# Evacuating the output with one 64-partition copy per engine, and storing it as 128 rows of 256 B

## The chip, the cores and the metric

One core of a Trainium2 chip. The metric is the device time of one execution in microseconds (us); a kernel's time is the median of its runs. TensorE multiplies, VectorE and ScalarE copy, and SyncE (SP) issues the loads and the store: the "issue" is its instruction that starts a transfer, the "landing" the transfer's last semaphore update. SBUF and PSUM are the core's own memories (the products end up in PSUM), DRAM is the memory outside it. Where a time is compared, it is with runs of the kernel before on the same chip in the same rounds.

## The reference, cut to what matters

One decoding step of attention for 32 sequences. Each reads the last 512 positions of its key and value caches, and the result goes through an output projection:

```python
q = (x @ wq) ...                       # x: [32, 1, 512]
p = softmax(q . k * Dh**-0.5)          # 8 kv heads, 512 positions, Dh = 128
o = p . v
return o.reshape(32, 1, 4096) @ wo     # out: [32, 1, 512] in bf16, 32 KB
```

The kernel reads 75.5 MB and writes 32 KB. The change is about these 32 KB.

## The kernel before: the parts that matter

```python
oT_flat = oT_sb[:, :, :].rearrange("p h b -> p (h b)")
x_sb = oT_flat[0:32, 0:D]
out_sb = x_sb.rearrange("b (c n) -> b c n", c=4)      # 32 partitions x 4 x 128
...
# SyncE (SP): the last loads, then the store
for hg in range(NHG):
    sp.dma_start(wo_sb[:, hg]..., wo[...]...).then_inc(sem_wo[hg], 16)
sp.wait_ge(dve_out, 2)
sp.wait_ge(act_out, 2)
sp.dma_start(out.rearrange("b s n -> b (s n)"),
             out_sb[:, :, :].rearrange("b c n -> b (c n)")).then_inc(sem_out, 16)
sp.wait_ge(sem_out, 16)
...
# TensorE: four column tiles, so output columns 128c .. 128c+127 land on partitions 32c .. 32c+31
for hg in range(NHG):
    pe.wait_ge(sem_wo[hg], 16)
    for i in range(4):
        for c in range(4):
            ins = pe.matmul(X_ps[32*c:32*(c+1), 2, 0:128], lhsT=o_sel[:, i, hg, :],
                            rhs=wo_sb[:, hg, i, c*128:(c+1)*128], ..., tile_position=(0, 32*c))
ins.then_inc(pe_fin, 1)
...
# VectorE; ScalarE does the same for c = 2, 3 with activation(Copy)
dve.wait_ge(pe_fin, 1)
for c in range(2):
    dve.tensor_copy(out_sb[:, c, :], X_ps[32*c:32*(c+1), 2, 0:128]).then_inc(dve_out, 1)
```

The four copies do two things: they bring the result out of PSUM, and they move the four groups of 32 partitions next to each other, so that one sequence's 512 columns lie in one partition and the store has 32 rows of 1024 B.

## Time and profile before

| | before |
|---|---|
| time | 188.11 us (188.02 to 188.25, 3 runs); 188.06 over 6 runs |
| span of the profiled run | 185.9 us |
| end of the last product | 183.35 us |
| from there to the end ("the tail") | 2.60 us |

The prediction shows the slices, the end of the chain, the timeline of the tail and the issue times. Two more lines of the page are needed. The first counts all DMA packets (its counts "under" a size are cumulative), the second is the store: kilobytes, and us from the start of the issue to landing.

```profile
DMA packets 6160, 75.80 MB, mean 408 GB/s; under 512 B 704, under 2 KB 768, under 8 KB 1792
...
out_dram<-oT_sb SPq DMA_DIRECT2D x1, 32.0 KB, 1.5
```

The 704 packets under 512 B are all semaphore writes of 4 B, 16 for each of 44 transfers. The packet records do not name a DMA engine; as in the prediction, 16 such writes are taken to stand for 16 engines.

### The profile page before, as it was taken

To read this page: it belongs to the slowest core of one execution; us is meant where nothing else is said; L and a number is where in the kernel's file an instruction comes from. 1 tells how busy PE (TensorE), PEld (TensorE's weight loads), DVE (VectorE), ACT (ScalarE), POOL (GpSimd) and SP (SyncE) were. 2 spreads that over 40 slices of the span, in tenths; PEclk is the share of its full clock that TensorE was granted. 3 is DMA by queue.
4 is the path that set the end of the run, shared out by engine and by line. 5 is a ranking of instruction groups with operands and counts; after the bars stand their busy time and mean duration, and the time that the engine had idled before them with its cause. 6 is when DMAs were issued, how large, how long until landed. Compare 5 with 4: busy or idle time off the path is not lost.

```text
span 185.9 us, 3841 instructions
## 1 busy us (share of the span) xinstructions
PE 110.3 (59%) x1604; PEld 90.7 (49%) x1604; DVE 131.8 (71%) x239; ACT 82.4 (44%) x142; POOL 32.1 (17%) x82
## 2 busy tenths in 40 slices
PE   0232004346179925949726992459699975999851
PEld 0100001032069804929326881129669974999741
DVE  0006999689999799985899959999999993010001
ACT  3001000259420199011992039826989999711011
POOL 7100390500700071050420060000030000000000
PEclk9999999999999995796955899657999999699999
DMA  6999999999999999999999999999999999999980
GB/s 208 419 444 423 430 430 419 444 423 426 426 419 430 426 419 430 434 419 434 418 430 430 423 434 412 441 430 416 432 416 430 423 430 426 423 430 404 401 326 25
DMA packets 6160, 75.80 MB, mean 408 GB/s; under 512 B 704, under 2 KB 768, under 8 KB 1792
## 3 DMA queue, kind: packets, MB, share of 16 engines
q1 hardware_dynamic: 6096, 75.53, 96.2%
q8 instruction: 12, 0.20, 0.4%
q10 hardware_dynamic: 48, 0.03, 0.1%
q14 instruction: 4, 0.03, 0.0%
HBM read 75.53 MB, written 0.03 MB: 406 GB/s over the span
## 4 chain that ended last, share of the span: by engine, by line
DMA 58%; DVE 22%; PE 11%; issue 4%; SPq 3%; ACT 0%; DVEq 0%
DMA V_sb<-in_v_cache_dram 31%; DVE KT_sb L426 14%; DMA w_sb<-in_wo_dram 12%; DMA K_sb<-in_k_cache_dram 8%; PE O_ps L353 7%; DMA w_sb<-in_wq_dram 6%; DVE w_sb L448 4%; DVE QA_sb L416 2%; PE S_ps L316 2%; SPq L211 2%; PE X_ps L296 1%; PE PT_ps L335 1%; SPq L200 1%; DVE oT_sb L409 0%; DVE KT_sb L404 0%
## 5 line engine op out<-in xcount | busy, mean ns | idle before, releaser
L426 DVE STREAM_TRANSPOSE KT_sb<-K_sb 128x2048 uint32<-128x2048 uint32 x32 | 72.3, 2287 | 1.2 <-DMA K_sb<-in_k_cache_dram 1.1
L353 PE MATMUL O_ps<-w_sb,V_sb 128*128 128x128 bf16 x640 | 46.1, 241 | 10.5 <-DMA V_sb<-in_v_cache_dram 5.6
L353 PEld LDWEIGHTS O_ps<-w_sb,V_sb 128*128 128x128 bf16 x640 | 44.7, 109 | 13.7 <-issue 7.0
L265 POOL COPY QBD<-QA_sb 32x64 bf16<-32x64 bf16 x64 | 25.6, 540 | 79.6 <-PE S_ps L316 62.0
L515 ACT ACTIVATE w_sb<-PTc,mask 128x512 bf16<-128x512 bf16 x60 | 38.9, 729 | 0.0
L316 PE MATMUL S_ps<-KT_sb,QBD 128*32 128x512 bf16 x256 | 20.9, 479 | 26.3 <-DVE KT_sb L426 19.8
L448 DVE TENSOR_SCALAR w_sb<-PTc,mask 128x512 bf16<-128x512 bf16 x100 | 30.2, 370 | 4.9 <-PE O_ps L353 4.9
L316 PEld LDWEIGHTS S_ps<-KT_sb,QBD 128*32 128x32 bf16 x256 | 7.8, 110 | 35.9 <-issue 32.0
L487 ACT ACTIVATE X_ps<-S_ps,negmax 128x512 f32<-128x512 f32 x8 | 5.3, 659 | 42.2 <-DVE negmax L435 42.2
L335 PE MATMUL PT_ps<-P_bf,pick 128*128 128x128 bf16 x128 | 11.8, 265 | 18.0 <-ACT P_bf L496 14.7
L335 PEld LDWEIGHTS PT_ps<-P_bf,pick 128*128 128x128 bf16 x128 | 10.2, 122 | 20.9 <-ACT P_bf L496 16.3
L525 ACT ACTIVATE oT_sb<-O_ps 128x128 bf16<-128x128 f32 x8 | 6.0, 750 | 26.0 <-PE O_ps L353 26.0
L515 ACT ACTIVATE K_sb<-PTc,mask 128x512 bf16<-128x512 bf16 x24 | 15.3, 717 | 1.6 <-DVE KT_sb L426 1.6
L353 PE MATMUL O_ps<-K_sb,V_sb 128*128 128x128 bf16 x256 | 15.1, 217 | 1.3 <-DMA V_sb<-in_v_cache_dram 1.0
L353 PEld LDWEIGHTS O_ps<-K_sb,V_sb 128*128 128x128 bf16 x256 | 14.5, 96 | 2.1 <-issue 1.3
L448 DVE TENSOR_SCALAR K_sb<-PTc,mask 128x512 bf16<-128x512 bf16 x40 | 12.1, 377 | 0.3 <-ACT PTc L506 0.2
L353 PE MATMUL O_ps<-KT_sb,V_sb 128*128 128x128 bf16 x128 | 9.1, 240 | 2.4 <-DMA V_sb<-in_v_cache_dram 2.4
L353 PEld LDWEIGHTS O_ps<-KT_sb,V_sb 128*128 128x128 bf16 x128 | 8.9, 108 | 2.5 <-issue 2.5
L469 DVE CAST K_sb<-S_ps 128x256 bf16<-128x256 f32 x1 | 0.4, 424 | 12.7 <-PE S_ps L365 12.7
L515 ACT ACTIVATE KT_sb<-PTc,mask 128x512 bf16<-128x512 bf16 x12 | 7.8, 725 | 0.0
L467 DVE CAST K_sb<-X_ps 128x384 bf16<-128x384 f32 x1 | 0.6, 558 | 9.8 <-PE X_ps L365 9.8
L496 ACT ACTIVATE P_bf<-X_ps,recip 128x512 bf16<-128x512 f32 x8 | 5.5, 685 | 4.4 <-DVE recip L441 4.4
(41 smaller groups left out, 49.5 us busy)
## 6 DMA issues: line engine op xcount, KB each, us to landing
K_sb<-in_k_cache_dram SPq DMA_DIRECT2D x16, 2048.0 KB, 15.2
V_sb<-in_v_cache_dram SPq DMA_DIRECT2D x16, 2048.0 KB, 17.0
w_sb<-in_wq_dram SPq DMA_DIRECT2D x2, 2048.0 KB, 9.7
w_sb<-in_wo_dram SPq DMA_DIRECT2D x8, 512.0 KB, 20.3
oT_sb<-in_x_dram ACTq DMA_DIRECT2D x1, 32.0 KB, 4.5
out_dram<-oT_sb SPq DMA_DIRECT2D x1, 32.0 KB, 1.5
```

The costliest lines, as they stand in the source:

```text
L211: sp.dma_start(wo_sb[:, hg].rearrange("p i n -> p (i n)"), wo[hg * 512:(hg + 1) * 512, :].rearrange("(m i) n -> m (i n)", i=4),).then_inc( ...
L265: pool.tensor_copy(dst[:, i, :, x0:x0 + 4], src).then_inc(pool_qbd, 1)
L316: ins = pe.matmul(S_ps[32 * c:32 * c + 32, q % 2, :], lhsT=QBD[:, q % 2, g, b, e, :], rhs=bass.AP(tensor=KT_sb, offset=s0 * slot + (b * G ...
L335: ins = pe.matmul(PT_ps[:, r, :], lhsT=pick[:, r, KS - s:KS - s + P], rhs=P_bf[:, s, :], start=(s == 0), stop=(s == KS - 1), tile_position ...
L353: ins = pe.matmul(O_ps[:, q % 2, 0:P], lhsT=V_sb[:, m % NV, r, :], rhs=z_of(q)[:, :, x0 + r, :], start=(e == 0 and r == 0), stop=(e == 1 a ...
L416: dve.tensor_copy(QA[32 * a:32 * a + 32, c], QW[32 * c:32 * c + 32, :, :, a::4].rearrange("p h k q -> p h q k"),).then_inc(dve_q, 1)
L426: dve.transpose(KT_w[:, n % NK, b].rearrange("p i r s -> p r i s"), K_w[:, n % NK, :, 32 * b:32 * b + 32],).then_inc(dve_T, 1)
L448: ins = dve.tensor_scalar(z_of(q)[:, k].rearrange("p x r -> p (x r)"), PTc[:, q % RING].rearrange("p x r -> p (x r)"), mask[:, k:k + 1], N ...
L487: act.activation(P_f32, S_ps[:, q % 2, :], ACTF.Exp, bias=negmax[:, q:q + 1], scale=SCALE, accum_out=sums[:, q:q + 1],).then_inc(act_exp, 1)
L496: act.activation(P_bf[:, :, :], P_f32.rearrange("p (x s) -> p s x", s=KS), ACTF.Copy, scale=recip[:, q:q + 1],).then_inc(act_P, 1)
L515: ins = act.activation(z_of(q)[:, k].rearrange("p x r -> p (x r)"), PTc[:, q % RING].rearrange("p x r -> p (x r)"), ACTF.Copy, scale=mask[ ...
L525: act.activation(oT_sb[:, :, 4 * q:4 * q + 4].rearrange("p h a -> p a h"), O_ps[:, q % 2, 0:P].rearrange("p (a h) -> p a h", a=4), ACTF.Co ...
```

## The change

Its intent: each engine evacuates its two groups of 32 partitions with one operation of 64, since the copies of this trace take their time from the columns and not from the partitions (on VectorE 280 ns for 32 partitions by 128 columns, 291 ns for 128 by 128). The result then stays on 128 partitions, and the store has to put it in order: 128 rows of 256 B, with a DRAM side that counts c (4), then b (32).

```diff
-        out_sb = x_sb.rearrange("b (c n) -> b c n", c=4)
+        out_sb = oT_flat[:, 0:P]
@@
-            sp.wait_ge(dve_out, 2)
-            sp.wait_ge(act_out, 2)
+            sp.wait_ge(dve_out, 1)
+            sp.wait_ge(act_out, 1)
             sp.dma_start(
-                out.rearrange("b s n -> b (s n)"), out_sb[:, :, :].rearrange("b c n -> b (c n)")
+                out.rearrange("b s (c n) -> c b (s n)", c=4), out_sb
             ).then_inc(sem_out, 16)
@@
-            for c in range(2):
-                dve.tensor_copy(
-                    out_sb[:, c, :], X_ps[32 * c:32 * (c + 1), 2, 0:128]
-                ).then_inc(dve_out, 1)
+            dve.tensor_copy(out_sb[0:64, :], X_ps[0:64, 2, 0:128]).then_inc(dve_out, 1)
@@
-            for c in range(2, 4):
-                act.activation(
-                    out_sb[:, c, :], X_ps[32 * c:32 * (c + 1), 2, 0:128], ACTF.Copy
-                ).then_inc(act_out, 1)
+            act.activation(out_sb[64:128, :], X_ps[64:128, 2, 0:128], ACTF.Copy).then_inc(act_out, 1)
```

## The prediction

> **What bounds the kernel now.** I read the page's forty slices first, then the chain that ended last, then the timeline of the last microseconds, then the waits of the DMA queue, and last the issue times. The slices say that almost the whole kernel is one stream of loads:
>
> ```profile
> DMA  6999999999999999999999999999999999999980
> GB/s 208 419 444 423 430 430 419 444 423 426 426 419 430 426 419 430 434 419 434 418 430 430 423 434 412 441 430 416 432 416 430 423 430 426 423 430 404 401 326 25
> ...
> HBM read 75.53 MB, written 0.03 MB: 406 GB/s over the span
> ```
>
> From the second slice to the 38th the transfers run at 400 to 440 GB/s. Nothing the change touches lies there. Only the last slice (25 GB/s, 4.65 us long as 185.9/40) is free of loads, and the whole change is inside it. The end of the chain that ended last:
>
> ```profile
> 159.94 22.96 DMA w_sb<-in_wo_dram
> 182.90 0.04 issue
> 182.94 0.44 PE X_ps L388 x16
> 183.38 0.02 issue
> 183.40 0.28 DVE oT_sb L472
> 183.68 0.31 DVEq L71
> ```
>
> The last piece of the output weights lands, sixteen products follow, then the output is evacuated. The chain is cut off at the evacuation by the profile's inference (span 185.9, it stops at 183.99), so the rest comes from the timeline and the waits:
>
> ```profile
> 183.40 0.56 ACT L542 ACTIVATE oT_sb<-X_ps 32x128 bf16<-32x128 f32 x2 [5.94 <-PE X_ps L388]
> 183.40 0.59 DVE L472 CAST oT_sb<-X_ps 32x128 bf16<-32x128 f32 x2 [4.79 <-PE X_ps L388]
> 184.06 0.35 SPq L217 DMA_DIRECT2D out_dram<-oT_sb  x1
> ...
> SPq L71 <- DMA out_dram<-oT_sb: 1.1, 1, 1.1
> ```
>
> So the tail is strictly serial: products end 183.35, two copies on each engine until 183.99, the store is issued 184.06 to 184.41, it lands 1.5 us after its issue began (the page's DMA part), and 0.35 us of closing semaphores end the span. Anything saved or added here moves the end one for one; it is 2.5 us of 185.9.
>
> **What the Trainium skill says.** (1) "Perfetto Trace Analysis", section "Optimizing Scalar/DVE Operations": each VectorE or ScalarE instruction carries a fixed data-access overhead, so fewer, larger ones are better. The trace agrees for the free size: CAST out of PSUM takes 280 ns for 128 columns and 558 ns for 384, so 1.09 ns a column and some 140 ns fixed. (2) "DMA: Bandwidth & Descriptors", section "Why a DMA increments its semaphore by 16 and not by 1": a DMA is split over the largest number k of engines, at most 16, that divides the outermost dimension of both its sides. The trace agrees where k should be 16: the store of before (32 rows on both sides) has 32 data packets and 16 semaphore packets. The new store's DRAM side is written c, b, n with c = 4 outermost, and its SBUF side has 128 partitions, so the rule gives k = 4. No transfer of the kernel before has such a small outermost dimension, so no run here shows it yet. (3) The same page, "Specifications", says that transfers under 512 B make the DMA read, modify and write. Rows of 256 B fall under that; no data packet of before is under 1024 B, so the trace says nothing. (4) The same page, "Anatomy of one DMA", says that the semaphore waits for the receipt of the last write. The trace agrees: by its packet records the store's last data packet ends at 185.21 and its semaphore is complete at 185.55.
>
> **Part one, the evacuation: -0.30 us.** Two instructions of 32 partitions become one of 64 on each engine. Does one of 64 partitions cost more?
>
> ```profile
> L472 DVE CAST oT_sb<-X_ps 32x128 bf16<-32x128 f32 x2 | 0.6, 280 | 4.8 <-PE X_ps L388 4.8
> ...
> L400 DVE CAST oT_sb<-X_ps 128x128 bf16<-128x128 f32 x1 | 0.3, 291 | 5.7 <-PE X_ps L283 5.7
> ```
>
> The same cast on all 128 partitions took 291 ns against 280 on 32, so I take 285 for 64. ScalarE: 270 ns for 32x128; its 128x384 copy took 490, and 256 more columns at the 0.84 ns a column of its 128x512 and 128x384 copies (597 - 490 over 128) explain 215 of the 220 ns between, so partitions cost it nothing either. Both pairs of copies ran side by side; the later pair member is VectorE's, starting 0.31 us after the first. One copy of 0.285 instead of 0.59 saves 0.305 us, all of it ahead of the store: -0.30.
>
> **Part two, the issue: +0.18 us.** The store's issue goes from a plain 32-row pattern to a three-dimensional one with 128 rows.
>
> ```profile
> L200 SPq DMA_DIRECT2D K_sb<-in_k_cache_dram x16: 534/535/696, 1.7 to 108.7; - x16
> ...
> L211 SPq DMA_DIRECT2D w_sb<-in_wo_dram x8: 432/432/8570, 156.5 to 159.9; - x8
> ...
> L217 SPq DMA_DIRECT2D out_dram<-oT_sb x1: 355/355/355, 184.1 to 184.1; - x1
> ```
>
> Columns are min/median/max in ns. 32 plain rows take 355, 128 plain rows 432, 128 rows with a source of two outer dimensions (the K cache) 535. The new store is of the last kind: 535 - 355 = +0.18.
>
> **Part three, the transfer: +0.42 us.** By the packet records of before, the store's 32 packets of 1024 B take 46 ns or more each and lie between 184.91 and 185.21, 0.29 us in all, two to an engine. The loads' packets of 4096 B take 160 ns, so (160 - 46)/3072 = 0.037 ns a byte, and a packet of 256 B would take 46 - 768 x 0.037 = 18 ns; with the 3 to 5 ns seen between packets, some 21 (an estimate). With k = 4 each of four engines has 32 of them: 32 x 21 = 0.67, with the semaphore's packet 0.70 us. 0.70 - 0.29 = +0.41; I write +0.42 for rounding and the start of four engines. The wait before the first packet (0.50 us after the issue ended) and the receipt (0.34) I leave as they are.
>
> **The sum.** -0.30 + 0.18 + 0.42 = +0.30 us, so 188.11 + 0.30 = 188.4 us. Everything before 183.35 is unchanged: the same loads in the same order, the same buffers; the staging tile moves from 32 partitions to 128 of the same tile, which by then has been read for the last time.
>
> **The rivals.** *The saving shows and the store costs nothing more.* If the program spreads the store over 16 engines in spite of its outermost 4, each has 8 packets of about 21 ns, 0.17, plus the same stagger: about 0.3 as now. Then -0.30 + 0.18 = -0.12, 188.0 us; if the issue too stays at 432, 187.9. For it speaks that the K cache's source also has a split outer dimension and still ran on 16 engines (6160 packets in all are 16 for each of 44 transfers, one per row, and 16 of instruction fetches); against it, that one's outermost count is 32, which 16 divides. *Small writes are slow.* If a 256 B write is a read, modify and write and takes as long as a 1024 B one (44 to 78 ns, mean near 57), 32 in a row take 1.8 us instead of 0.70, and the sum is +1.4: 189.5. For it speaks only the skill's line; the trace has no small data packet. *Noise decides.* The three timed runs of before lie within 0.23 us and the profiled one gave 187.66, 0.45 below their median: the streaming part of 180 us varies by as much as the effect, so the sign seen may not be the change's.
>
> **Range and chances.** Low end: the 16-engine rival, 187.9. High end: packets of about twice my size, which adds 0.7 to 0.8 us, so 189.2. The change acts on 2.5 us of the span; 2% would be 3.8 us, more than removing the whole tail could give and more than twice my worst mechanism. So within 2% nearly surely; 0.01 for slower in case the store stalls in a way that no line shows.
>
> **What would show it right or wrong.** In the profile after: one CAST and one ACTIVATE of 64x128 of 280 to 290 and about 270 ns; the store's issue 0.3 us after the products end, lasting about 535 ns; 132 packets instead of 48 in the store (page total 6244, under 512 B 820) if k = 4, but 144 (6256 and 832) if k = 16; landing about 2.1 us after issue instead of 1.5; transfers at the end showing a DMA share near 4/16. The prediction is wrong in its direction if the landing stays at 1.5 to 1.7 us, and in its size if 256 B packets take over 40 ns each. It would be wrong altogether if the granted clock or the load stream changed, which nothing in the diff does.

## The result, and the profile after

188.30 us (188.03 to 188.49, 6 runs) against 188.06 (187.94 to 188.25, 6 runs). The ratio is 1.0011, 95% interval 0.9998 to 1.0023: within 2%, and on times alone the sign is not told, since the interval reaches below 1. Ratios here are the mean time of one kernel's runs over that of the other's of the same rounds, so not quite the ratio of the medians quoted.

The end of the timeline of the changed kernel (start, us, engine, line, operation):

```profile
183.29 0.41 PE L388 MATMUL X_ps<-w_sb,K_sb 128*32 128x128 bf16 x16 [0.83 <-DMA w_sb<-in_wo_dram]
183.75 0.27 ACT L538 ACTIVATE oT_sb<-X_ps 64x128 bf16<-64x128 f32 x1 [6.28 <-PE X_ps L388]
183.75 0.28 DVE L471 CAST oT_sb<-X_ps 64x128 bf16<-64x128 f32 x1 [5.13 <-PE X_ps L388]
184.11 0.69 SPq L217 DMA_DIRECT2D out_dram<-oT_sb  x1
```

One copy each, of the length that one of 32 partitions had; the store is issued 0.41 us after the products' end (183.70) instead of 0.71. But the issue itself lasts 0.69 us instead of 0.355. Its packets and its landing on the page of the changed kernel:

```profile
DMA packets 6244, 75.80 MB, mean 406 GB/s; under 512 B 820, under 2 KB 852, under 8 KB 1876
...
out_dram<-oT_sb SPq DMA_DIRECT2D x1, 32.0 KB
```

6244 and 820 are the numbers of the prediction for four engines: 128 rows and only 4 semaphore packets. The landing time is missing, because the page counts 16 semaphore updates for a landing and only 4 engines send one. In the trace a single early update stands for the rest, 1.48 us after the products, long before the first engine's own (2.53). A stretch of the same kernel holds the whole transfer (the last columns are the mean granted clock, the mean busy share of 16 DMA engines, and GB/s):

```profile
184.80:185.40 0.60, 0.00 (x0) 0.00 (x0) 0.00 (x0) 0.00 (x0) 0.00 (x0) 1.00 0.00 0
185.40:186.00 0.60, 0.00 (x0) 0.00 (x0) 0.00 (x0) 0.00 (x0) 0.00 (x0) 0.63 0.24 55
```

The share of 0.24 looks like 4/16 but tells nothing of the number of engines: 128 packets of 18 ns are 0.24 of 16 times 0.60 us however they are spread, and the run e2 below, with 16 semaphore packets, has 0.25 in such a stretch. What does tell is the order of the packets: in the middle of this store they start in fours, one four every 14 ns (at 1.871, 1.871, 1.873 and 1.877 us after the products, then at 1.885, 1.885, 1.887 and 1.891), as four engines would. And the queue waits longer for it than the 1.1 us of before (the sum, times, longest):

```profile
SPq L71 <- DMA out_dram<-oT_sb: 1.5, 1, 1.5
```

With the packet records and semaphore updates of both traces, the tail can be cut into pieces (us; zero is the end of the last product):

| | before | after | difference | predicted |
|---|---|---|---|---|
| products' end to start of the issue | 0.706 | 0.414 | -0.292 | -0.30 |
| start of the issue to first packet | 0.859 | 1.294 | +0.435 | +0.18 |
| first packet to end of the last row | 0.290 | 0.540 | +0.250 | +0.42 |
| last row to last semaphore update | 0.347 | 0.331 | -0.016 | 0 |
| closing | 0.395 | 0.398 | +0.003 | 0 |
| tail | 2.597 | 2.977 | +0.380 | +0.30 |

The two spans differ by 0.73 us, not 0.38: the products end at 183.35 in one profile and 183.70 in the other. That is not the change. In the ten experiments below, all with the same loads, they ended anywhere from 183.18 to 183.65, without order. So the tail is read from the profile, and the times say only how big the whole is.

### The profile page after: what moved, and what is told of

It is laid out like the page before. It is cut to its first block, busy times and chain, and to the rows that moved or that the text cites. A ratio compares the mean times of both kernels' runs of the same rounds, so it can differ in the third digit from the quotient of the medians.

```text
span 186.7 us, 3839 instructions
## 1 busy us (share of the span) xinstructions
PE 110.8 (59%) x1604; PEld 91.0 (49%) x1604; DVE 131.5 (70%) x238; ACT 81.9 (44%) x141; POOL 32.1 (17%) x82
## 2 busy tenths in 40 slices
DMA packets 6244, 75.80 MB, mean 406 GB/s; under 512 B 820, under 2 KB 852, under 8 KB 1876
## 4 chain that ended last, share of the span: by engine, by line
DMA 56%; DVE 25%; PE 10%; issue 3%; SPq 3%; DVEq 0%
DMA V_sb<-in_v_cache_dram 31%; DVE KT_sb L426 15%; DMA w_sb<-in_wo_dram 12%; PE O_ps L353 7%; DMA w_sb<-in_wq_dram 7%; DMA K_sb<-in_k_cache_dram 6%; DVE w_sb L448 6%; DVE QA_sb L416 2%; PE S_ps L316 2%; SPq L211 2%; PE X_ps L296 1%; DVE maxv L433 1%; SPq L200 1%; DVE oT_sb L409 0%; DVE KT_sb L404 0%
## 5 line engine op out<-in xcount | busy, mean ns | idle before, releaser
L353 PE MATMUL O_ps<-w_sb,V_sb 128*128 128x128 bf16 x640 | 46.7, 243 | 10.2 <-DMA V_sb<-in_v_cache_dram 5.0
L353 PEld LDWEIGHTS O_ps<-w_sb,V_sb 128*128 128x128 bf16 x640 | 45.3, 110 | 13.3 <-DVE w_sb L448 6.7
```

The costliest lines, as they stand in the source:

```text
L353: ins = pe.matmul(O_ps[:, q % 2, 0:P], lhsT=V_sb[:, m % NV, r, :], rhs=z_of(q)[:, :, x0 + r, :], start=(e == 0 and r == 0), stop=(e == 1 a ...
```

## The experiments

**The theory:** the tail is serial and its parts add. The copies give 0.29; the store takes back more, in two separate ways: its pattern has a second outer dimension, which delays the first packet, and it runs on four engines, which lengthens the transfer. **Rivals:** rows of 256 B are slow to write in themselves; the second dimension is harmless and the few engines do all the harm; the saving of the copies was never real. Here is the outcome; then each run (us; columns as in the table above, ratios of times against the kernel before).

| run | issue starts | to first packet | packets | to last update | tail | time ratio (95%) |
|---|---|---|---|---|---|---|
| before | 0.71 | 0.86 | 0.29 | 0.35 | 2.60 | 1 |
| after | 0.41 | 1.29 | 0.54 | 0.33 | 2.98 | 1.0011 (0.9998 to 1.0023) |
| e1_store_only | 0.70 | 1.30 | 0.54 | 0.33 | 3.27 | 1.0035 (1.0020 to 1.0051) |
| e5_one_copy_old_store | 0.41 | 0.86 | 0.29 | 0.35 | 2.30 | 0.9982 (0.9967 to 0.9997) |
| e2_flat_rows | 0.41 | 0.85 | 0.26 | 0.35 | 2.26 | 0.9975 (0.9963 to 0.9987) |
| e8_outer16 | 0.41 | 1.29 | 0.28 | 0.36 | 2.72 | 1.0010 (0.9995 to 1.0025) |
| e9_outer8 | 0.42 | 1.36 | 0.31 | 0.34 | 2.83 | 1.0017 (1.0002 to 1.0032) |
| e7_plain_k4 | 0.71 | 0.78 | 1.29 | 0.33 | 3.51 | 1.0058 (1.0040 to 1.0075) |
| e6_padded_rows | 0.71 | 1.34 | 0.34 | 0.35 | 3.14 | 1.0030 (1.0016 to 1.0045) |
| e4_two_stores | 0.36, 0.36 | 1.25 | 0.98 | 0.32 | 3.32 | 1.0031 (1.0015 to 1.0047) |
| e3_four_stores | 0.36 to 0.77 | 0.86 | 0.68 | 0.49 | 2.78 | 1.0004 (0.9992 to 1.0016) |
| e10_two_halves | 0.41, 0.73 | 0.86 | 0.52 | 0.35 | 2.53 | 1.0004 (0.9992 to 1.0016) |

Where there are several stores, "to first packet" is from the earliest issue of SyncE, and "packets" spans all of them.

### The store alone (e1_store_only)

```diff
-            dve.tensor_copy(out_sb[0:64, :], X_ps[0:64, 2, 0:128]).then_inc(dve_out, 1)
+            for c in range(2):
+                dve.tensor_copy(
+                    out_sb[32 * c:32 * (c + 1), :], X_ps[32 * c:32 * (c + 1), 2, 0:128]
+                ).then_inc(dve_out, 1)
 # ScalarE the same for c = 2, 3; SyncE waits for 2 and 2
```

> The new store alone, with the two 32-partition copies per engine of before. I call the time from the end of the last product to the end of the span the tail: 2.60 us before, 2.98 after. My theory (the parts add up in series): the second copies come back, the issue starts 0.70 us after the products instead of 0.41, all that follows is as in the changed kernel, tail 3.27 us, time about 188.06 + 0.67 = 188.7 us. Rival (the saved copy was worth nothing because the store's landing is set by something else): tail 2.98 as after, 188.3 us.

188.54 us against 187.87. The timeline's end of this run:

```profile
183.60 0.59 DVE L472 CAST oT_sb<-X_ps 32x128 bf16<-32x128 f32 x2 [5.07 <-PE X_ps L388]
183.60 0.56 ACT L542 ACTIVATE oT_sb<-X_ps 32x128 bf16<-32x128 f32 x2 [6.23 <-PE X_ps L388]
184.25 0.69 SPq L217 DMA_DIRECT2D out_dram<-oT_sb  x1
```

The tail is 3.267 us where 3.27 was expected. The store alone costs 0.67 us, shown by the trace and by the times (0.35% of 187.9 is 0.66).

### The evacuation alone (e5_one_copy_old_store)

Wrong result: half of the stored columns hold stale data.

```diff
 # the kernel before
-            for c in range(2):
+            for c in range(1):
                 dve.tensor_copy(out_sb[:, c, :], ...
 # ScalarE: range(2, 3); SyncE waits for 1 and 1
```

> Wrong result on purpose: the kernel before with its second copy on each engine left out and its own store of 32 rows of 1024 B, that is the evacuation's saving alone. My theory: the store's issue starts 0.41 us after the products instead of 0.71, everything after it as before, tail 2.60 - 0.29 = 2.31 us, time 0.29 us under before (0.15%). Rival (something other than the copies holds the store back): tail 2.60, time as before.

187.54 us against 187.73; the tail is 2.300. The end of its timeline, to be compared with that of the kernel before in the prediction:

```profile
183.40 0.27 ACT L542 ACTIVATE oT_sb<-X_ps 32x128 bf16<-32x128 f32 x1 [5.94 <-PE X_ps L388]
183.40 0.28 DVE L472 CAST oT_sb<-X_ps 32x128 bf16<-32x128 f32 x1 [4.78 <-PE X_ps L388]
183.76 0.35 SPq L217 DMA_DIRECT2D out_dram<-oT_sb  x1
```

The saving of the copies is real and goes to the end in full: 0.30 us. That, with the 0.67 of the run before, is the whole change: 2.60 - 0.30 + 0.67 = 2.97, and 2.977 was measured.

### Small rows in plain order (e2_flat_rows)

Wrong result: the rows go to DRAM in the order of the partitions.

```diff
-                out.rearrange("b s (c n) -> c b (s n)", c=4), out_sb
+                out.rearrange("b s (c n) -> (b s c) n", c=4), out_sb
```

> Wrong result on purpose: the changed kernel with its 128 rows of 256 B stored in flat order, so that the store's DRAM side is one plain dimension of 128. My theory (four engines and the three-dimensional issue cost the time): 144 store packets, 16 per-engine receipts, issue about 0.43 us instead of 0.69, packets within 0.3 us instead of 0.54, landing about 1.6 us after issue, tail about 2.4 us, time about 187.8 us. Rival (rows under 512 B are slow to write, whatever the engines): packets well over 18 ns each or a late receipt, landing about 2.1 us, tail about 2.9 us, time 188.3 us.

187.42 us against 187.87, and the tail is 2.263, even shorter than expected. The issue (minimum, median and maximum in ns) and the landing (us) of this store, and the packets:

```profile
L217 SPq DMA_DIRECT2D out_dram<-oT_sb x1: 348/348/348, 184.1 to 184.1; - x1
...
DMA to landing us min/median/max: 1.5/1.5/1.5
...
DMA packets 6256, 75.80 MB, mean 408 GB/s; under 512 B 832, under 2 KB 864, under 8 KB 1888
```

128 rows of 256 B on 16 engines are issued as fast as 32 rows of 1024 B (355 ns) and land as fast; the packets take 18 ns and lie within 0.26 us. This refutes the rival of slow small writes, and also a guess of the prediction: that 128 rows alone lengthen an issue. It also shows what the change could have won: 0.33 us, if the rows lay in a plain order.

### Two dimensions, 16 engines (e8_outer16) and 8 engines (e9_outer8)

Wrong result: another order of rows, but the same form as the changed kernel's store. These two separate the second dimension from the number of engines.

```diff
-                out.rearrange("b s (c n) -> c b (s n)", c=4), out_sb
+                out.rearrange("(h g) s (c n) -> (g c) h (s n)", g=4, c=4), out_sb   # 16 by 8; e9: g=2, 8 by 16
```

> Wrong result on purpose: the changed kernel with the rows stored in another order, so that the DRAM side counts 16 by 8 rows instead of 4 by 32: two outer dimensions as in the changed kernel, but 16 engines. My theory (both the second outer dimension and k below 16 cost issue time, and k = 4 alone costs transfer time): issue about 0.53 us as in the K loads, 144 store packets within 0.3 us, landing about 1.7 us after issue, tail about 2.45 us, 187.7 us. Rival (the outermost count does not matter, the two dimensions do): issue 0.69, tail 2.9.

> Wrong result on purpose: as the run with 16 by 8, but 8 by 16 rows, so k = 8 by the rule: 136 store packets, 16 rows an engine at 14 ns, packets within about 0.3 us, issue about 0.69 us if any k below 16 costs the same extra step, about 0.6 if it grows with what is missing to 16; tail about 2.7 us, 188.0 us. Rival (few engines are no cost): same tail as with 16 by 8.

Of the run with 16 by 8, then of the one with 8 by 16, the store's issue, and how many packets (16 by 8 also has its landing):

```profile
L217 SPq DMA_DIRECT2D out_dram<-oT_sb x1: 626/626/626, 184.0 to 184.0; - x1
...
DMA to landing us min/median/max: 1.9/1.9/1.9
...
DMA packets 6256, 75.80 MB, mean 407 GB/s; under 512 B 832, under 2 KB 864, under 8 KB 1888
```

```profile
L217 SPq DMA_DIRECT2D out_dram<-oT_sb x1: 751/751/751, 183.8 to 183.8; - x1
...
DMA packets 6249, 75.80 MB, mean 407 GB/s; under 512 B 825, under 2 KB 857, under 8 KB 1881
```

With 16 engines, 144 packets and all else as in the plain order, the issue is 626 ns instead of 348, and the first packet comes 1.286 us after its start instead of 0.853: the second dimension costs 0.43 us. With 8 engines it is 1.355, with 4 (the changed kernel) 1.294: no trend with the number of engines. The packets then lie within 0.28, 0.31 and 0.54 us for 16, 8 and 4 engines. Could it be the order of the rows in DRAM, which leaves gaps between them, and not the second dimension? The stores of e3 and e10 below speak against that: their rows do not touch either (they start 1024 B apart), but they are counted in one dimension, and SyncE's first store in each is issued in 355 ns with its first packet after 0.86 us, as in the kernel before. So of what the store costs, 0.43 us are the form and 0.25 the four engines, and neither rival "only the engines" nor "only the form" stands.

My expectations for these runs were short: I expected 2.45 and 2.7 us of tail and got 2.72 and 2.83, as I had the issue of 16 by 8 too short (0.53 us; it was 0.63) and had not seen that the first packet comes later by more than the issue is longer. For 8 engines the page counts 6249 packets, one more than 136 over the 6112 of everything else; by the packet records the store has its 128 rows and 8 semaphore packets, so the odd one belongs elsewhere.

### Four engines in one dimension (e7_plain_k4)

Wrong result.

```diff
 # the kernel before
-                out.rearrange("b s n -> b (s n)"), out_sb[:, :, :].rearrange("b c n -> b (c n)")
+                out.rearrange("(r b) s n -> r (b s n)", r=4), K_0[0:4, 0:4096]
```

> Wrong result on purpose: the kernel before with its store replaced by one of 4 plain rows of 8 KB, so four engines but one dimension. If running on fewer than 16 engines is what lengthens the issue: issue 0.5 us or more and an early update of the semaphore. If the second outer dimension is what lengthens it: issue 0.35 us. The transfer itself has one 8 KB row an engine, about 0.31 us. Tail 2.6 to 2.8 us, time 188.0.

The issue:

```profile
L217 SPq DMA_DIRECT2D out_dram<-K_sb x1: 347/347/347, 184.1 to 184.1; - x1
```

347 ns and 0.78 us to the first packet: fewer than 16 engines do not lengthen the issue, although an early semaphore update is seen here too, 1.17 us after the products. The transfer I had wrong by far: each row of 8 KB took 1.0 us (8.2 GB/s an engine), not 0.31, so the tail was 3.51 us and the time 188.82 against 187.73. Why one such row is so slow, this run does not settle: all four rows come out of SBUF partitions 0 to 3 and moved at 25.5 GB/s together (32 KB in 1.29 us), so a limit that these neighbouring partitions share would fit as well as one of each engine. The comparison of issues does not hang on it.

### Two dimensions on the SBUF side (e6_padded_rows)

```diff
 # the kernel before
-        out_sb = x_sb.rearrange("b (c n) -> b c n", c=4)
+        out_sb = oT_flat[0:32, 0:640].rearrange("b (c n) -> b c n", c=4)[:, :, 0:128]
-                out.rearrange("b s n -> b (s n)"), out_sb[:, :, :].rearrange("b c n -> b (c n)")
+                out.rearrange("b s (c n) -> b (s c) n", c=4), out_sb
```

> The kernel before with its 32 rows of output staged 320 B apart instead of 256, so that the same store reads four runs of 256 B in each partition: two dimensions on the SBUF side, outermost 32, 16 engines, correct result. If any second dimension costs what it cost on the DRAM side (16 by 8: 1.29 us from issue start to first packet against 0.85 plain): issue 0.62 us, first packet 1.29 us after its start, 144 store packets, tail about 3.0 us, 188.2 us. If only a DRAM side with a second dimension costs it: issue 0.35 us, tail 2.6 us, as before.

188.22 us against 187.70, correct. The issue and the landing:

```profile
L217 SPq DMA_DIRECT2D out_dram<-oT_sb x1: 677/677/677, 183.9 to 183.9; - x1
...
DMA to landing us min/median/max: 2.0/2.0/2.0
```

677 ns, and 1.34 us to the first packet: with the gaps on the SBUF side a second dimension costs about the same, with the evacuation of before and 16 engines. (The DRAM side of this run is written 32 by 4 too, though without gaps, so the run does not separate the two sides strictly.) The tail is 3.14 us, 0.54 over before.

### Two stores of two chunks (e4_two_stores)

```diff
+ # SyncE, after VectorE's copy: out[c = 0, 1] from partitions 0 to 63
+                out.rearrange("b s (c n) -> c b (s n)", c=4)[0:2], out_sb[0:64, :]
+ # ScalarE, after its own copy: out[c = 2, 3] from partitions 64 to 127
+                out.rearrange("b s (c n) -> c b (s n)", c=4)[2:4], out_sb[64:128, :]
```

> The changed kernel's evacuation with its store in two halves, one from SyncE and one from ScalarE, each with an outermost count of 2, so by the rule on 2 engines; correct result. Each engine then has 32 rows as in the changed kernel. My theory (the rows per engine set the transfer): packets over 0.5 us or more again, 130 store packets if the two halves use different or the same two engines, over 0.9 us if both halves queue on the same two engines; issue between 0.5 and 0.7 us; tail 2.8 to 3.0 us or about 3.3 if the same engines serve both; time 188.2 to 188.7. Rival (the issue's length depends on how many rows one instruction has): issue near 0.5 us and tail 2.7 or less, 188.1 us.

188.51 us against 187.87, tail 3.32. Both issues:

```profile
L539 ACTq DMA_DIRECT2D out_dram<-oT_sb x1: 1096/1096/1096, 183.9 to 183.9; - x1
...
L216 SPq DMA_DIRECT2D out_dram<-oT_sb x1: 671/671/671, 183.9 to 183.9; - x1
```

128 rows and 4 semaphore packets, within 0.98 us. The packet records give each half two chains of rows at 14 to 15 ns. ScalarE's lie between 1.615 and 2.138 us after the products, SyncE's between 2.121 and 2.596, and each of SyncE's two chains begins within 6 ns of the start of the semaphore packet that closes one of ScalarE's (2.115 and 2.121; 2.134 and 2.135). So both halves very likely ran on the same two engines, one after the other, the case that was expected at 3.3; the records do not name the engines. SyncE's issue is no shorter for half the rows, and ScalarE's, begun 8 ns earlier, lasts 1.10 us.

### Four plain stores (e3_four_stores): can the order be mended?

```diff
+ # SyncE, after VectorE's copy, c = 0, 1; ScalarE, after its own copy, c = 2, 3:
+                out[:, 0, 128 * c:128 * (c + 1)], out_sb[32 * c:32 * (c + 1), :]     # 32 rows of 256 B each
```

> The changed kernel's evacuation with four stores of 32 rows of 256 B, two issued by SyncE after VectorE's copy, two by ScalarE after its own copy; correct result. My theory: each store has a plain 32-row pattern, runs on 16 engines (192 store packets in all), issues in 0.36 to 0.41 us; the second of a pair is issued by about 1.2 us after the products, lands at about 2.1, tail about 2.5 us, so 0.1 under before and 0.5 under after, time about 187.95 us. Rival (small rows are slow, or four stores get in each other's way): second landing at 2.3 or later, tail 2.7 or more, 188.2 us or more.

187.95 us against 187.87 (ratio 1.0004), correct. Both engines' issues end the timeline:

```profile
183.67 0.86 ACTq L541 DMA_DIRECT2D out_dram<-oT_sb  x2
183.68 0.82 SPq L217 DMA_DIRECT2D out_dram<-oT_sb  x2
```

Each store is plain and ran on 16 engines (128 rows, 64 semaphore packets). But the tail is 2.78 us, not 2.5, which is the number written down for the rival that the stores get in each other's way: the second pair's packets start 0.92 us after its issue, and its last semaphore update comes 0.49 us after the last row instead of 0.35; the 32 updates of that pair arrive one after another, about half of them 5 to 6 ns apart. What delays them is not shown. Better than the changed kernel by 0.2 in the tail, but no better than the kernel before.

### Two stores, the first under the second copies (e10_two_halves)

```diff
 # the kernel before; VectorE copies c = 0, 2; ScalarE c = 1, 3
-            sp.wait_ge(dve_out, 2)
-            sp.wait_ge(act_out, 2)
+            sp.wait_ge(dve_out, 1)
+            sp.wait_ge(act_out, 1)
+                out[:, 0, 0:256], out_sb[:, 0:2, :].rearrange("b c n -> b (c n)")       # SyncE
+ # ScalarE, after both engines' second copies:
+                out[:, 0, 256:512], out_sb[:, 2:4, :].rearrange("b c n -> b (c n)")
```

> A correct version meant to beat both: the two copies per engine of before, but in the order that completes columns 0 to 255 first, stored from SyncE as 32 plain rows of 512 B while the second copies run, and columns 256 to 511 stored by ScalarE after them. From the plain stores seen so far (0.78 to 0.86 us from issue start to first packet, under 0.3 us of packets, 0.34 us to the last receipt): second issue at 0.66 us, first packet 1.52, last receipt about 2.06, tail about 2.46 us, 0.14 under before, 187.7 if before runs at 187.87 us. Rival, from the run with four stores (two queues at once delay each other): last receipt 2.2 to 2.3, tail 2.6 to 2.7, no gain.

187.66 us against 187.70, correct; ratio 1.0004. The tail is 2.534, 0.06 under before instead of 0.14, as ScalarE begins its issue only at 0.73:

```profile
183.76 0.35 SPq L217 DMA_DIRECT2D out_dram<-oT_sb  x1
184.09 0.33 ACTq L547 DMA_DIRECT2D out_dram<-oT_sb  x1
```

One profile shows the 0.06 and the times do not, so no correct version was found that beats the kernel before beyond the noise.

## Why the prediction was right, step by step

- **What bounds the kernel, and that the change lies in the serial tail:** right. The copies' saving and the store's cost came out in the tail undiminished, alone (e5: -0.30, e1: +0.67) and together (+0.38).
- **The evacuation, -0.30:** right. 64 partitions took 283 ns on VectorE and 272 on ScalarE; the issue starts 0.292 us earlier.
- **Four engines:** right. The packet counts were those written down for k = 4 (k is the number of engines), and the packets start in fours. The third sign that the prediction named, a DMA share near 4/16, could not have told (0.24 here, 0.25 in e2).
- **"Part two, the issue: +0.18 us":** mis-sized. From the start of the issue to the first packet it was +0.435. The prediction took the issue's length from the K loads (535 ns; it was 690) and left the time from the issue's end to the first packet as it was (0.50 us; it was 0.60). It also put part of the increase down to 128 rows, and e2 shows that they cost nothing. What e8 and e6 show is one cost of 0.43 to 0.48 us for a second outer dimension, with the gaps between rows on the DRAM side (e8) or on the SBUF side (e6).
- **"Part three, the transfer: +0.42 us":** mis-sized the other way, +0.250. The packets took the estimated 18 ns, but follow each other every 14, so 32 take 0.45 us where the prediction had 21 ns each; the rest of the 0.54 us goes to their not keeping step (their semaphore packets lie up to 48 ns apart) and to the less regular first rows.
- **The sum:** +0.30 predicted and +0.38 in the tail; 188.4 predicted and 188.30 measured. That the sum fits better than its terms is luck: the two errors, +0.26 and -0.17, mostly cancel. The last semaphore update came 2.17 us after the issue began, where 2.1 was written down.
- **The rivals:** that noise decides came true for the times (0.9998 to 1.0023); the sign rests on the tails (+0.38), to which the two parts measured alone (e1 and e5, intervals clear of 1) add up. The slow small write is refuted by e2. The 16-engine rival did not happen, and e8 shows that it would not have brought 188.0 as written, but a tail 0.13 above before.
- **Readings that were off, without consequence:** the tail is 2.60 us and not 2.5, as the closing takes 0.395 us and not 0.35; the last slice is not free of loads, since it begins at 181.3 and the last weights land at 182.90; "the store's issue 0.3 us after the products end" should have been 0.41 by the prediction's own sum; the 1024 B packets take 44 ns or more, not 46. The section cited under (4) describes transfers issued from GpSimd; for these stores from SyncE the measured 0.35 us stands.
- **Open:** why the issue's length varies among such stores (626, 690 and 751 ns for 16, 4 and 8 engines), each seen in one or two profiles; why ScalarE's issue in e4 lasts 1.10 us; and what delays the second pair in e3.

## What to carry to other kernels

Before rearranging a store to save a copy, write down the pattern of both its sides: how many outer dimensions each has, and what divides the outermost. Here a second dimension cost 0.43 us and an outermost count of 4 another 0.25, against 0.29 saved by halving the copies, while the size of the rows (256 B instead of 1024 B) cost nothing. In a tail that is serial, each such term can be read from one profile to within some hundredths of a microsecond, when the times differ by less than their own noise.

## What the Trainium skill lacked or had wrong

- "DMA: Bandwidth & Descriptors", "Why a DMA increments its semaphore by 16 and not by 1": the rule for k held in every run (4 by 32 rows: 4 semaphore packets; 8 by 16: 8; 16 by 8: 16). The section gives no time for a small k: here 32 rows of 256 B on each of 4 engines lay within 0.54 us, every 14 ns on an engine, and 8 on each of 16 engines within 0.28.
- No page that I read gives the cost of a second outer dimension in a DMA's pattern: 0.43 us (e8 against e2) and 0.48 (e6 against before) from the start of the issue to the first packet.
- The same page, "Specifications", has a read-modify-write for transfers under 512 B. For 128 rows of 256 B on 16 engines the runs show no cost of it in the time to landing: packets of 18 ns, 1.46 us to landing against 1.50 for rows of 1024 B. Whether a read-modify-write took place, no run shows.
- The same page, "Anatomy of one DMA", divides a DMA's fixed 2 us for the GpSimd path alone, and puts most of it down to the write receipt. The section has no such division for stores from SyncE: here 0.35 us of 1.50 passed between the last row and the last semaphore update, and 0.86 us before the first packet.
